# Tiles 4 to 9: half of g turned by TensorE instead of in blocks; queries and keys of batch 3 turned by VectorE

## The chip, the core and the metric

The kernel runs on one core of one Trainium2 chip. The metric is the device time of one execution in microseconds. Five engines work at once, each through its own instruction stream in order: TensorE (PE; its weight loads are PEld), VectorE (DVE), ScalarE (ACT), GpSimd (POOL) and SyncE (SP), which here issues nearly all DMAs.

## The reference

Three parts follow each other: attention of a global and a banded local part, a dense expert, and a soft mixture of 8 experts. All data are float32.

```python
# attention: batch 4, heads 8, 512 local and 32 global positions, head 64
s_g  = scale * q_g @ concat(k_g, k_l).T          # global queries see everything
s_ll = scale * q_l @ k_l.T, kept where |i - j| <= 32
s_lg = scale * q_l @ k_g.T                       # local queries: band and global keys
x = concat(softmax(s_g) @ v, softmax(s_lg, s_ll) @ v)     # (2176, 512)
# dense expert
h = x @ w_in ; g = max(0.01 h, h) ; y = g @ w_out         # 512 -> 2048 -> 512
# soft mixture: 8 experts with 4 slots each
logits = y @ phi                                  # (2176, 32)
d = softmax over tokens ; c = softmax over slots
slots = d.T @ y ; out = c @ expert_mlp(slots)     # w1, relu, w2 for each expert
```

## The kernel before

The 2176 tokens are 17 tiles of 128 (0 to 15 local, four for each batch; 16 holds the global ones). For a tile `b_X` turns the attention output, and `b_H(t, f)` computes a quarter f of h by 12 matmuls of 512 columns (`hp`) and writes g through ScalarE. The logits of a tile need g turned (contraction over its 2048 columns). There are two ways for that:

- `b_L(t, f)`: TensorE transposes a quarter of g in four 128x128 pieces (`gtp`), VectorE or ScalarE brings it to `gT`.
- `blocks(t, f, gs)`, for the tiles in `BLK` (4 to 14): VectorE transposes each quarter in 32x32 blocks (L703, `gb<-g`), and for each two quarters 16 copies of 32x256 move the blocks to their places (L712). `MOVE` gives all 16 of the first half (f 0 and 1) to GpSimd and shares those of the second half (f 2 and 3): 6 GpSimd, 5 VectorE, 5 ScalarE.

Then comes the tile's chain of logits: `b_D1` copies the logits to `lp` (VectorE L744); `b_D2` sums them on TensorE (L750), VectorE takes the maximum (L754), ScalarE the exponential `st` (L759), VectorE copies a part of `st` (L760); `b_D3` transposes `st` on TensorE (L795) and VectorE makes `d` (L782); `b_U` multiplies `d` with g (`up`, L805), and VectorE adds that to `uacc` (L810).

`l_items` lists these steps. `b_items` sets the steps of tile t - 1 between the half quarters of H of tile t. Where t - 1 is in `BLK`, D1 stands behind the second quarter, and three halves of H stand between D2 and D3. Where it isn't, `b_L` stands there first, D1 comes later, and one half of H stands between D2 and D3.

Attention goes by 16 pairs (b, i) of two heads. `load_qk` loads queries and keys (`qn`, `kn`, two buffers each). `a_T` has TensorE transpose each in four pieces (`kTp`, `qTp`), ScalarE brings them to `kT` (four buffers, kept until the global softmax `g_S` has read them) and `qT` (two; with the scale), and VectorE copies the windows `kw` (L403, L404). `a_S` computes scores (`sc`), VectorE adds the mask and takes maxima (L444), ScalarE takes exponentials (L452); `a_E` transposes these (`etp`) and VectorE copies them to `eT` (L473); `a_V` multiplies with values (`vw`), whose global rows GpSimd copies (L200). The steps of attention for batches 2 and 3 are merged with the H of tiles 4 to 10. `gtp`, `kTp`, `qTp`, `etp` and `xtp` share two PSUM banks ("tp"), `sc` and the `gl` of `g_S` two others.

The order on each engine is not that of the code: a scheduler sets it at build, with a time model of its own, so an edit in one place can move rows in others.

Of the kernel before, what the change touches and what calls it, by code (L numbers as in the profile page):

```python
# [8 lines left out]
F32 = mybir.dt.float32  # L9
# [11 lines left out]
def kernel(  # L21
# [15 lines left out]
    nc = tc.nc  # L37
    B, H, S, D = q_l.shape
# [3 lines left out]
    P = 128  # L42
# [5 lines left out]
    NTT = B * NT + 1  # L48
# [10 lines left out]
    def bank(tag, name, bufs):  # L59
        return ps.tile([P, 512], F32, tag=tag, name=name, bufs=bufs)  # L60

    def tp(name):
        return bank("tp", name, 2)
# [93 lines left out]
    def load_qk(b, i, ts=(None, None)):  # L157
        for src, nm, t in ((k_l, "kn", ts[0]), (q_l, "qn", ts[1])):
            if t is None:
                t = sa.tile([P, NT, 2, D], F32, tag=nm, name=nm, bufs=2)  # L160
            for h in range(2):
                nc.sync.dma_start(
                    out=t[:, :, h, :], in_=src[b, 2 * i + h].rearrange("(t p) d -> p t d", p=P)
                )
            nat[nm, b, i] = t
# [215 lines left out]
    def a_T(b, i):  # L381
        qn, kn = nat.pop(("qn", b, i)), nat.pop(("kn", b, i))
        for src, dst, nm, bf in ((kn, kT, "kT", 4), (qn, qT, "qT", 2)):
            pt = tp(nm + "p")
            if b == 0:
                warm(pt)
            for T in range(NT):
                nc.tensor.transpose(
                    pt[:, P * T:P * T + P], src[:, T].rearrange("p h d -> p (h d)"), ident
                )  # L390
            t = sa.tile([P, S], F32, tag=nm, name=nm, bufs=bf)
            nc.scalar.activation(  # L392
                out=t, in_=pt, func=AF.Copy, scale=scale if nm == "qT" else 1.0,
            )
            dst[b, i] = t
        kt = kT[b, i]
        HW = NW // 2
        kwin[b, i] = []
        for hf in range(2):
            kw = sa.tile([P, HW, P], F32, tag="kw", name="kw", bufs=3)  # L400
            src = kt[:, 32 * HW * hf:32 * HW * hf + 96]
            src = bass.AP(src.tensor, src.offset, [src.ap[0], [32, HW], [1, 96]])
            nc.vector.tensor_copy(kw[:, :, 0:96], src)  # L403
            nc.vector.tensor_copy(  # L404
                kw[:, :, 96:128],
                kgT[:, i, 32 * b:32 * b + 32].unsqueeze(1).to_broadcast([P, HW, 32]),
            )
            kwin[b, i].append(kw)
# [7 lines left out]
    def a_S(b, i):  # L416
# [3 lines left out]
        sm = sa.tile([P, NT, 2], F32, tag="sm", name="sm", bufs=2)  # L420
        rs = sa.tile([P, NT, 2], F32, tag="rs", name="rs", bufs=2)
        es = []
        bks = [bank("sc", f"sc{e}", 2) for e in range(2)]
        if b == 0:
            for bk in bks:
# [12 lines left out]
        for e in range(2):  # L438
            bk = bks[e]
            s = sa.tile([P, S + SG], F32, tag="se", name="se", bufs=4)[:, 0:S].rearrange(  # L440
                "p (t k) -> p t k", t=NT
            )
            for T in range(NT):
                nc.vector.tensor_tensor_reduce(  # L444
                    out=s[:, T, :], in0=bk[:, P * T:P * T + P],
                    in1=mask[:, 0 if T == 0 else 2 if T == NT - 1 else 1, :],
                    scale=1.0, scalar=-3.0e38, op0=ALU.add, op1=ALU.max,
                    accum_out=mx[:, e, T:T + 1],
                )
            nc.vector.tensor_scalar_mul(nmx[:, e], mx[:, e], -1.0)  # L450
            for T in range(NT):
                exp_last[0] = nc.scalar.activation(  # L452
                    out=s[:, T, :], in_=s[:, T, :], func=AF.Exp,
                    bias=nmx[:, e, T:T + 1], accum_out=sm[:, T, e:e + 1],
                ).ins
            es.append(s)
        nc.vector.tensor_scalar_add(sm, sm, 1e-9)
# [182 lines left out]
    gt = {}  # L640
    ms = {}
    seq = [(b, T) for b in range(B) for T in range(NT)] + [None]
    BLK = range(4, NTT - 2)
    MOVE = "P" * 16, "PPPPPPDDDDDAAAAA"
    gp = []

# [22 lines left out]
    def b_H(t, f, half=None):  # L669
# [10 lines left out]
        w = wi[f]  # L680
# [8 lines left out]
            return  # L689
        gs = gt[t][:, 512 * f:512 * f + 512]  # L690
        nc.scalar.activation(out=gs, in_=hp, func=AF.Prelu, alpha=0.01)  # L691
        if t in BLK:
            blocks(t, f, gs)

    gbl = {}
# [20 lines left out]
    def b_L(t, f, ev=None):  # L716
        g = gt[t]
        pt = tp("gtp")
        for c in range(4):
            o = 512 * f + P * c  # L720
            nc.tensor.transpose(pt[:, P * c:P * c + P], g[:, o:o + P], ident)  # L721
        gT = part("gT")
        (ev or (nc.vector.tensor_copy if f % 2 and not (t >= 6 and f in (1, 3, 9)) else nc.scalar.copy))(
            gT, pt
        )
        lst[t, f] = gT.rearrange("p (c t) -> p c t", c=4)
# [135 lines left out]

    def l_items(t):
        return ([(0.0, lambda: None), (0.6, lambda: b_M(t, range(2)))] if t in BLK else [
            (0.9, lambda: (b_L(t, 0), b_L(t, 1))),
            (0.9, lambda: (b_L(t, 2), b_L(t, 3))),
        ]) + [
            (1.3, lambda: b_D1(t)),
            (0.3, lambda: b_D2(t)),
            (0.1, lambda: b_D3(t)),  # L870
            (1.0, lambda: b_U(t)),
        ]
# [454 lines left out]
```

## Time and profile before

| what | value |
|---|---|
| median of 3 runs | 519.07 us (516.73 to 519.13) |
| the profiled execution's own time | 516.28 us |
| its span, first to last instruction | 514.2 us |
| TensorE busy | 464.5 us, 90% of the span |
| VectorE, ScalarE, GpSimd busy | 301.2, 248.7, 181.1 us |
| mean granted TensorE clock | 0.962 |

The span is the profiled execution without what lies around it (2.1 us). Busy time of TensorE counts matmuls that are pipelined, so it is not the share of its peak. The granted clock is 1 at 2.4 GHz and 0.5 at 1.2 GHz. Attention of batches 2 and 3 with tiles 4 to 9 lies at about 205 to 345 us, the tiles without attention at 345 to 450 us, and the mixture behind that.

### The profile page before, as it was taken

What the parts mean: (1) busy time and instruction counts of PE and PEld (TensorE: products, weight loads), DVE (VectorE), ACT (ScalarE), POOL (GpSimd) and SP (SyncE); (2) the same over time, 40 slices, a digit from 0 to 9 for tenths busy, and PEclk for the clock granted to TensorE, in tenths of its full rate; (3) what the DMA queues carried; (4) which work ended last, traced back from release to release, by engine and by line L of the source; (5) the groups of instructions that cost most, each with busy time, mean ns of one, the idle gap of its engine ahead of it and who ended that gap; (6) DMA issues with size and microseconds to landing.
All of it is one profiled execution on the core that took longest, in us unless ns stands there. A gap on an engine that the chain in (4) does not pass through costs nothing.

```text
span 514.2 us, 13727 instructions
## 1 busy us (share of the span) xinstructions
PE 464.5 (90%) x5279; PEld 322.2 (63%) x5279; DVE 301.2 (59%) x996; ACT 248.7 (48%) x762; POOL 181.1 (35%) x345
## 2 busy tenths in 40 slices
PE   8976988978999989689898899999999999999994
PEld 5644766556775657456675667677777777633353
DVE  4586769759576663866766975656555541312422
ACT  4787878759654163444525473144433442300222
POOL 2066688443202015206263636516656620000000
PEclk9978899979998999879999999999999999999998
DMA  9998767799755750602480500229620059999987
GB/s 178 235 231 229 212 216 297 209 303 275 189 116 107 169 114 1 131 8 56 127 149 9 108 8 0 84 83 399 256 83 2 0 196 342 385 378 377 302 249 207
DMA packets 122397, 90.25 MB, mean 176 GB/s; under 512 B 75804, under 2 KB 101212, under 8 KB 122332
## 3 DMA queue, kind: packets, MB, share of 16 engines
q1 hardware_dynamic: 119660, 88.33, 60.2%
q10 hardware_dynamic: 2672, 1.05, 0.8%
q8 instruction: 41, 0.67, 0.6%
q14 instruction: 24, 0.20, 0.1%
HBM read 76.68 MB, written 8.65 MB: 166 GB/s over the span
## 4 chain that ended last, share of the span: by engine, by line
PE 60%; DVE 13%; ACT 7%; DMA 5%; issue 3%; POOL 2%; SPq 0%; ACTq 0%; POOLq 0%; DVEq 0%
PE hp L684 29%; PE ehp L1167 3%; PE up L805 3%; PE lg L735 3%; ACT se L452 2%; PE gtp L721 2%; PE sc L432 2%; DMA rraw<-in_moe_w_out_dram 2%; DVE se L444 2%; DMA rraw<-in_moe_w_in_dram 2%; PE po L489 2%; PE sop L1243 1%; POOL wn L259 1%; PE etp L471 1%; PE sop L1221 1%
## 5 line engine op out<-in xcount | busy, mean ns | idle before, releaser
L684 PE MATMUL hp<-wi,xxh 128*128 128x512 f32 x512 | 166.5, 407 | 7.1 <-ACT g L691 3.6
L712 POOL COPY g<-gb 32x256 f32<-32x256 f32 x242 | 97.6, 403 | 95.8 <-DVE gb L703 37.5
L684 PEld LDWEIGHTS hp<-wi,xxh 128*128 128x128 f32 x512 | 92.8, 191 | 41.2 <-issue 12.0
L684 PE MATMUL hp<-wi,xxl 128*128 128x512 f32 x256 | 101.5, 397 | 0.0
L452 ACT ACTIVATE se<-se,nmx 128x128 f32<-128x128 f32 x128 | 49.6, 390 | 24.2 <-DVE nmx L450 21.4
L691 ACT ACTIVATE g<-hp 128x512 f32<-128x512 f32 x60 | 35.7, 594 | 47.6 <-PE hp L684 46.9
L684 PEld LDWEIGHTS hp<-wi,xxl 128*128 128x128 f32 x256 | 48.7, 190 | 12.1 <-issue 0.8
L703 DVE STREAM_TRANSPOSE gb<-g 128x512 f32<-128x512 f32 x44 | 30.9, 706 | 19.4 <-ACT g L691 19.0
L200 POOL COPY vw<-vw 32x1664 f32<-32x1664 f32 x10 | 15.7, 1574 | 70.1 <-DMA vw<-in_v_g_dram 39.2
L259 POOL TENSOR_TENSOR wn<-wn,rraw 128x256 int32<-128x256 int32 x32 | 26.3, 836 | 32.6 <-DMA rraw<-in_moe_w_in_dram 23.4
L432 PE MATMUL sc<-kw,qT 64*32 64x128 f32 x1024 | 29.3, 292 | 1.1 <-issue 0.7
L444 DVE CUSTOM_DVE_ANT_0 se<-sc,mask 128x128 f32<-128x128 f32 x128 | 28.7, 282 | 1.4 <-PE sc L432 1.2
L471 PE MATMUL etp<-identr,se 128*128 128x128 f32 x128 | 23.1, 301 | 5.3 <-ACT kT L392 4.0
L259 POOL TENSOR_TENSOR wo<-wo,rraw 128x256 int32<-128x256 int32 x23 | 18.1, 800 | 25.5 <-DMA rraw<-in_moe_w_out_dram 4.5
L712 ACT COPY g<-gb 32x256 f32<-32x256 f32 x55 | 22.1, 402 | 9.2 <-DVE cs L788 4.1
L489 PE MATMUL po<-vw,eT 128*32 128x64 f32 x1024 | 24.0, 227 | 2.4 <-DMA vw<-vw 1.5
L249 ACT ACTIVATE rraw<-rraw 128x256 int32<-128x256 uint32 x55 | 23.2, 435 | 5.9 <-DMA rraw<-in_moe_w_in_dram 5.1
L432 PEld LDWEIGHTS sc<-kw,qT 64*32 64x32 f32 x1024 | 20.2, 112 | 7.7 <-issue 4.0
L403 DVE COPY kw<-kT 128x672 f32<-128x672 f32 x32 | 19.2, 638 | 9.0 <-ACT kT L392 8.8
L759 ACT ACTIVATE st<-lg,nm 128x128 f32<-128x128 f32 (+1 forms) x16 | 6.0, 373 | 38.2 <-DVE nm L758 34.5
L489 PEld LDWEIGHTS po<-vw,eT 128*32 128x32 f32 x1024 | 18.4, 113 | 9.7 <-issue 7.3
L452 ACT ACTIVATION_READ_ACCUMULATOR se<-se,nmx 128x1 f32 x128 | 24.1, 188 | 0.0
(227 smaller groups left out, 818.1 us busy)
## 6 DMA issues: line engine op xcount, KB each, us to landing
ew<-in_moe_w_dram SPq DMA_DIRECT2D x23, 1024.0 KB, 8.6
rraw<-in_moe_w_in_dram SPq DMA_DIRECT2D x32, 256.0 KB, 3.6
vw<-in_v_l_dram SPq DMA_DIRECT2D x60, 112.0 KB, 3.5
rraw<-in_moe_w_out_dram SPq DMA_DIRECT2D x23, 256.0 KB, 5.3
ew<-in_moe_w_dram SPq DMA_DIRECT2D x9, 512.0 KB, 9.6
ew<-in_moe_w_dram SPq DMA_DIRECT2D x17, 256.0 KB, 5.6
wo_f<-wo SPq DMA_DIRECT2D x16, 256.0 KB, 3.4
vn<-in_v_l_dram SPq DMA_DIRECT2D x4, 1024.0 KB, 6.1
```

The lines of the kernel that those rows point to most:

```text
L249: nc.scalar.activation(out=m, in_=lo, func=AF.Copy, scale=2.0 ** -29)
L259: nc.gpsimd.tensor_tensor(out=di, in0=di, in1=m, op=ALU.add)
L403: nc.vector.tensor_copy(kw[:, :, 0:96], src)
L432: nc.tensor.matmul(bks[e][32 * u:32 * u + 32, P * T:P * T + P], qt[64 * e:64 * e + 64, 32 * U:32 * U + 32], kw[win(U) // (NW // 2)][64 * e ...
L444: nc.vector.tensor_tensor_reduce(out=s[:, T, :], in0=bk[:, P * T:P * T + P], in1=mask[:, 0 if T == 0 else 2 if T == NT - 1 else 1, :], sca ...
L452: exp_last[0] = nc.scalar.activation(out=s[:, T, :], in_=s[:, T, :], func=AF.Exp, bias=nmx[:, e, T:T + 1], accum_out=sm[:, T, e:e + 1],).ins
L471: nc.tensor.transpose(pt[:, P * T:P * T + P], es[e][:, T, :], ident)
L489: nc.tensor.matmul(pov[32 * u:32 * u + 32, T, e, :], ets[e][:, 32 * U:32 * U + 32], vw[:, win(U), e, :], start=True, stop=True,)
L684: nc.tensor.matmul(hp, a[:, k, :], w[c][:, k, :], start=(k == 0 and n == 0), stop=(k == KD - 1 and n == 2),)
L691: nc.scalar.activation(out=gs, in_=hp, func=AF.Prelu, alpha=0.01)
L703: nc.vector.transpose(out=gb[:, f % 2], in_=gs)
L712: copy(dst[32 * c:32 * c + 32, :, a], src[32 * a:32 * a + 32, :, c])
```

## The change

The set `BLK` now holds tiles 10 to 14. A new set `HALF` holds 4 to 9: there quarters 0 and 1 are still turned in blocks (all moves on GpSimd), and quarters 2 and 3 by `b_L`. These tiles now take the other order of steps in `b_items`.

For batch 3 the loads of queries and keys go in runs of 32 floats (128 bytes): eight 32-partition DMAs for a pair where four of 128 partitions with runs of 256 bytes stood. The tile then holds 32x32 blocks in such places that one VectorE transpose of 128x512 gives `kT` or `qT`; the four TensorE transposes and ScalarE's copy are gone. The scale that this copy gave to the queries moves into the exponential.

```diff
--- before.py
+++ after.py
@@ -158,7 +158,19 @@
         for src, nm, t in ((k_l, "kn", ts[0]), (q_l, "qn", ts[1])):
             if t is None:
                 t = sa.tile([P, NT, 2, D], F32, tag=nm, name=nm, bufs=2)
+            if b >= 3:
+                t = t.rearrange("p t h d -> p (t h d)").rearrange("p (w d) -> p w d", d=32)
             for h in range(2):
+                if b >= 3:
+                    for c in range(2):
+                        g = 64 * h + 32 * c
+                        nc.sync.dma_start(
+                            out=t[g:g + 32],
+                            in_=src[b, 2 * i + h, :, 32 * c:32 * c + 32].rearrange(
+                                "(w k) d -> k w d", k=32
+                            ),
+                        )
+                    continue
                 nc.sync.dma_start(
                     out=t[:, :, h, :], in_=src[b, 2 * i + h].rearrange("(t p) d -> p t d", p=P)
                 )
@@ -381,6 +393,11 @@
     def a_T(b, i):
         qn, kn = nat.pop(("qn", b, i)), nat.pop(("kn", b, i))
         for src, dst, nm, bf in ((kn, kT, "kT", 4), (qn, qT, "qT", 2)):
+            if b >= 3:
+                t = sa.tile([P, S], F32, tag=nm, name=nm, bufs=bf)
+                nc.vector.transpose(out=t, in_=src.rearrange("p w d -> p (w d)"))
+                dst[b, i] = t
+                continue
             pt = tp(nm + "p")
             if b == 0:
                 warm(pt)
@@ -420,6 +437,7 @@
         sm = sa.tile([P, NT, 2], F32, tag="sm", name="sm", bufs=2)
         rs = sa.tile([P, NT, 2], F32, tag="rs", name="rs", bufs=2)
         es = []
+        sc_q = scale if b >= 3 else 1.0
         bks = [bank("sc", f"sc{e}", 2) for e in range(2)]
         if b == 0:
             for bk in bks:
@@ -447,11 +465,11 @@
                     scale=1.0, scalar=-3.0e38, op0=ALU.add, op1=ALU.max,
                     accum_out=mx[:, e, T:T + 1],
                 )
-            nc.vector.tensor_scalar_mul(nmx[:, e], mx[:, e], -1.0)
+            nc.vector.tensor_scalar_mul(nmx[:, e], mx[:, e], -sc_q)
             for T in range(NT):
                 exp_last[0] = nc.scalar.activation(
                     out=s[:, T, :], in_=s[:, T, :], func=AF.Exp,
-                    bias=nmx[:, e, T:T + 1], accum_out=sm[:, T, e:e + 1],
+                    bias=nmx[:, e, T:T + 1], scale=sc_q, accum_out=sm[:, T, e:e + 1],
                 ).ins
             es.append(s)
         nc.vector.tensor_scalar_add(sm, sm, 1e-9)
@@ -640,7 +658,8 @@
     gt = {}
     ms = {}
     seq = [(b, T) for b in range(B) for T in range(NT)] + [None]
-    BLK = range(4, NTT - 2)
+    BLK = range(10, NTT - 2)
+    HALF = range(4, 10)
     MOVE = "P" * 16, "PPPPPPDDDDDAAAAA"
     gp = []
 
@@ -689,7 +708,7 @@
             return
         gs = gt[t][:, 512 * f:512 * f + 512]
         nc.scalar.activation(out=gs, in_=hp, func=AF.Prelu, alpha=0.01)
-        if t in BLK:
+        if t in BLK or t in HALF and f < 2:
             blocks(t, f, gs)
 
     gbl = {}
@@ -862,7 +881,7 @@
 
     def l_items(t):
         return ([(0.0, lambda: None), (0.6, lambda: b_M(t, range(2)))] if t in BLK else [
-            (0.9, lambda: (b_L(t, 0), b_L(t, 1))),
+            (0.0, lambda: None) if t in HALF else (0.9, lambda: (b_L(t, 0), b_L(t, 1))),
             (0.9, lambda: (b_L(t, 2), b_L(t, 3))),
         ]) + [
             (1.3, lambda: b_D1(t)),
```

What moves in the order of instructions is shown at three places. Numbers behind a tile's name are buffers.

The first is TensorE at tile 3's chain of logits, while the scores of batch 2's last pair are computed. Before:

```order
L471 MATMUL etp<-identr,se 128x128 x8
L750 MATMUL lg<-lp,s_77 128x128
L388 MATMUL kTp<-identr,kn 128x128 x4
L388 MATMUL qTp<-identr,qn 128x128 x4
L471 MATMUL etp<-identr,se 128x128 x4
...
L795 MATMUL lg<-identr,st 128x128
...
L471 MATMUL etp<-identr,se 128x128 x2
L805 MATMUL up<-gx,d 32x512 x4
L684 MATMUL hp<-wi,xxh 128x512 x2
L684 MATMUL hp<-wi,xxl 128x512
```

`sc` are those scores, `etp` behind `qTp` the exponentials of the pair before. The change:

```order
L489 MATMUL etp<-identr,se 128x128 x8
L769 MATMUL lg<-lp,s_77 128x128
L405 MATMUL kTp<-identr,kn 128x128 x4
L405 MATMUL qTp<-identr,qn 128x128 x4
L740 MATMUL gtp<-identr,g 128x128 x4
L814 MATMUL lg<-identr,st 128x128
...
L450 MATMUL sc_3421<-kw,qT 32x128
L824 MATMUL up<-gx,d 32x512 x4
L703 MATMUL hp<-wi,xxh 128x512 x2
L703 MATMUL hp<-wi,xxl 128x512
L703 MATMUL hp<-wi,xxh 128x512 x2
L703 MATMUL hp<-wi,xxl 128x512
```

The second `etp` has gone behind, tile 4's `gtp` stands in its place, and the transpose of `st` and `up` come before most of the scores.

The second place is VectorE at tile 4's chain, from `lp` on, where batch 2's global softmax (`gmx`, `gnmx`) is computed too. Before:

```order
L744 COPY lp<-lg 128x128
L703 STREAM_TRANSPOSE gb<-g 128x512
L473 COPY eT<-etp 128x512
L661 SCALAR_TENSOR_TENSOR xxl<-xtp,xxh 128x512
L526 TENSOR_REDUCE gmx<-gl 128x1 x2
L754 TENSOR_REDUCE nm<-lg 128x1
L758 TENSOR_TENSOR nm<-nm 128x1
L527 TENSOR_REDUCE gmx<-gg 128x1
L763 TENSOR_TENSOR al<-nm 128x1
L527 TENSOR_REDUCE gmx<-gg 128x1
L528 TENSOR_REDUCE gnmx<-gmx 128x1
L760 COPY st<-lg 32x128
```

The change:

```order
L763 COPY lp<-lg 128x128
L420 COPY kw<-kT 128x7x96
L491 COPY eT<-etp 128x512
L398 STREAM_TRANSPOSE kT<-kn 128x512
L545 TENSOR_REDUCE gmx<-gg 128x1
L773 TENSOR_REDUCE nm<-lg 128x1
L545 TENSOR_REDUCE gmx<-gg 128x1
L398 STREAM_TRANSPOSE kT<-kn 128x512
L546 TENSOR_REDUCE gnmx<-gmx 128x1
L777 TENSOR_TENSOR nm<-nm 128x1
L546 TENSOR_REDUCE gnmx<-gmx 128x1
L515 TENSOR_TENSOR xn<-po,rs 128x4x128
```

Two key transposes of batch 3 and window copies now stand between `lp` and the second `nm`; the block transpose is gone.

The third place is TensorE at the same chain, from the matmul on `lp` (D2) to the transpose of `st` (D3). Before, two rows of H repeat where lines are left out:

```order
L750 MATMUL lg<-lp,s_77 128x128
L684 MATMUL hp<-wi,xxh 128x512 x2
L684 MATMUL hp<-wi,xxl 128x512
L521 MATMUL gg<-kgT,qgT 32x32 x8
L684 MATMUL hp<-wi,xxh 128x512 x2
L684 MATMUL hp<-wi,xxl 128x512
...
L489 MATMUL po<-vw,eT 32x64 x8
L388 MATMUL kTp<-identr,kn 128x128 x4
L388 MATMUL qTp<-identr,qn 128x128 x4
L489 MATMUL po<-vw,eT 32x64 x23
L795 MATMUL lg<-identr,st 128x128
L471 MATMUL etp<-identr,se 128x128 x8
```

The change:

```order
L769 MATMUL lg<-lp,s_77 128x128
L539 MATMUL gg<-kgT,qgT 32x32 x4
L507 MATMUL po<-vw,eT 32x64 x28
L450 MATMUL sc_3863<-kw,qT 32x128 x16
L489 MATMUL etp<-identr,se 128x128 x4
L450 MATMUL sc_3864<-kw,qT 32x128 x9
L489 MATMUL etp<-identr,se 128x128 x4
L814 MATMUL lg<-identr,st 128x128
L450 MATMUL sc_3864<-kw,qT 32x128 x7
L507 MATMUL po<-vw,eT 32x64 x4
L740 MATMUL gtp<-identr,g 128x128 x4
L450 MATMUL sc_4145<-kw,qT 32x128 x7
```

No `hp` is left between D2 and D3; the second half of the values, scores and `etp` stand there, and tile 5's `gtp` follows.

## Rows read from the trace of the kernel before

**Rows 1.** The page: busy microseconds, share of span and instructions of each engine.
```profile
PE 464.5 (90%) x5279; PEld 322.2 (63%) x5279; DVE 301.2 (59%) x996; ACT 248.7 (48%) x762; POOL 181.1 (35%) x345
```
**Rows 2.** Windows (us, engines' busy time with instructions, granted clock, DMA share, GB/s).
```profile
215.00:226.00 11.00, 6.95 (x85) 3.44 (x83) 8.52 (x40) 6.06 (x26) 3.53 (x7) 0.54 0.22 49
...
205.00:345.00 140.00, 126.70 (x1780) 89.99 (x1780) 95.83 (x326) 64.31 (x216) 56.87 (x123) 0.96 0.30 64
345.00:417.00 72.00, 72.00 (x480) 53.66 (x479) 41.22 (x110) 28.60 (x75) 44.12 (x110) 1.00 0.39 147
```
**Rows 3.** TensorE's waits, 210 to 350 us: total, times, longest.
```profile
PE etp L471 <- ACT kT L392: 4.0, 1, 4.0
...
PE up L805 <- DVE d L782: 1.6, 1, 1.6
PE lg L750 <- DMA vw<-in_v_l_dram: 1.5, 1, 1.5
```
**Rows 4.** TensorE in order of time: start, duration, work, and idle before it.
```profile
213.30 0.49 PE L750 MATMUL lg<-lp,s 128*128 128x128 f32 x2 [1.52 <-DMA vw<-in_v_l_dram]
...
219.86 1.11 PE L471 MATMUL etp<-identr,se 128*128 128x128 f32 x4 [4.05 <-ACT kT L392]
...
224.37 1.92 PE L805 MATMUL up<-gx,d 128*32 128x512 f32 x8
...
243.06 0.66 PE L388 MATMUL kTp<-identr,kn 128*128 128x128 f32 x4
243.55 0.60 PE L388 MATMUL qTp<-identr,qn 128*128 128x128 f32 x4
...
248.80 1.06 PE L805 MATMUL up<-g,d 128*32 128x512 f32 x8 [1.62 <-DVE d L782]
```
**Rows 5.** Costs by operation and shape, 205 to 345 us: busy, mean ns, idle before.
```profile
L703 DVE STREAM_TRANSPOSE gb<-g 128x512 f32<-128x512 f32 x23 | 16.0, 705 | 5.8 <-ACT g L691 5.4 <-ACT al L764 0.3
...
L712 DVE COPY g<-gb 32x256 f32<-32x256 f32 x30 | 13.0, 433 | 0.5
L712 ACT COPY g<-gb 32x256 f32<-32x256 f32 x30 | 12.1, 402 | 5.6 <-DVE nmx L450 3.9 <-DVE cs L788 1.4
...
L392 ACT ACTIVATE kT<-kTp 128x512 f32<-128x512 f32 x6 | 3.6, 593 | 4.1 <-PE kTp L388 4.1
...
L759 ACT ACTIVATE st<-lg,nm 128x128 f32<-128x128 f32 x6 | 2.2, 365 | 14.8 <-DVE nm L758 11.1 <-DVE gmx L527 3.7
...
L760 DVE COPY st<-lg 32x128 f32<-32x128 f32 x6 | 1.7, 284 | 1.7 <-ACT st L759 1.7
```
**Rows 6.** VectorE in order of time.
```profile
212.37 0.71 DVE L703 STREAM_TRANSPOSE gb<-g 128x512 f32<-128x512 f32 x1
...
215.02 1.18 DVE L450 TENSOR_SCALAR nmx<-mx 128x4 f32<-128x4 f32 x1
...
242.82 1.33 DVE L703 STREAM_TRANSPOSE gb<-g 128x512 f32<-128x512 f32 x2
...
244.50 1.21 DVE L403 COPY kw<-kT 128x672 f32<-128x672 f32 x2
...
248.76 1.27 DVE L473 COPY eT<-etp 128x512 f32<-128x512 f32 x2
```
**Rows 7.** ScalarE in order of time.
```profile
216.44 1.23 ACT L712 COPY g<-gb 32x256 f32<-32x256 f32 x3
...
219.23 0.57 ACT L392 ACTIVATE kT<-kTp 128x512 f32<-128x512 f32 x1
...
239.92 0.68 ACT L532 ACTIVATE gs<-gl,gnmx 128x512 f32<-128x512 f32 x1
```
**Rows 8.** The issue queue of SyncE, and how long key loads take to land.
```profile
207.72 4.09 SPq L191 DMA_DIRECT2D vw<-in_v_l_dram  x6
...
215.25 0.94 SPq L162 DMA_DIRECT2D kn<-in_k_l_dram  x2
...
DMA to landing us min/median/max: 2.3/2.7/3.5
```
**Rows 9.** GpSimd in order of time.
```profile
214.60 1.57 POOL L200 COPY vw<-vw 32x1664 f32<-32x1664 f32 x1 [9.17 <-DMA vw<-in_v_l_dram]
```

## The prediction

> **What bounds the kernel now.** The page's busy times come first: TensorE has 90% of the span, VectorE 59% [rows 1]. That is an average, so the windows come next. From 345 to 417 us TensorE is busy for all of 72.0 us at full clock; from 205 to 345 us, where the change sits, for 126.7 of 140 [rows 2]. So this stage holds 13.3 us in which TensorE stands, and each microsecond of TensorE's work that is added or taken away, or of standing that comes or goes, passes to the end: nothing behind it has slack. The list of TensorE's waits says what ends the standing: one wait of 4.0 us for ScalarE's copy of keys, one of 1.6 us for `d`, one of 1.5 us, then smaller ones [rows 3]. (The 1.5 us are put down to a DMA, but the matmul waits for VectorE's `lp`.) TensorE in order of time puts the largest close together: 1.52 us ahead of 213.30, some smaller ones, 4.05 us ahead of 219.86; the third is tile 4's `up` at 248.80 [rows 4]. The first group costs more than its idle time: from 215 to 226 us the granted clock is 0.54 [rows 2], and `up` there takes 1.92 us against 1.06 for the same columns at 248.80 [rows 4]. At 1.2 GHz lie some 6.3 us of work, from 219.86 to about 226.2; half of that, 3.2 us, is lost.
>
> So the group at 212 to 226 us costs about 6.3 us of idle (1.5 + 0.8 + 4.0) and 3.2 us of clock, tile 4's `up` 1.6 us, and the rest 13.3 - 6.3 - 1.6 = 5.4 us.
>
> **TensorE's own work.** `b_L` adds two groups of four transposes in each of six tiles, 12 groups; the four pairs of batch 3 lose two each, 8 groups. A group costs 0.49 us, from `kTp` at 243.06 to `qTp` at 243.55; up to 0.58 elsewhere [rows 4]. Four more groups: **+2.2 us** (1.9 to 2.4), all on the path.
>
> **The other engines' work.** VectorE loses in each of six tiles two block transposes of 0.705 us and five moves of 0.433, ScalarE five moves of 0.402 [rows 5], GpSimd six moves of about as much. VectorE gains eight transposes of queries and keys, costed as the same instruction on the same shape, 0.705 us, and two copies from PSUM (tiles 4 and 5) near 0.64 [rows 6]: -21.5 + 5.6 + 1.3 = -14.6 us. ScalarE gains ten such copies and loses eight, 0.593 each [rows 5]: -12.1 + 1.2 = -10.9 us. None of this counts by itself; it counts where TensorE's wait ends with that engine. The scale in the exponential is an operand of the same instruction: nothing (ScalarE's slack would hide a nanosecond on it anyway).
>
> **The stall at 212 to 226 us.** TensorE waits until ScalarE's `kT` copy at 219.23 frees a bank [rows 4, 7]. Ahead of that copy ScalarE does five of tile 4's moves and eight exponentials; three moves take 1.23 us, and four exponentials fill the 1.56 us from 217.67 to 219.23 [rows 7]. VectorE does two block transposes around `lp` and five moves [rows 5, 6]. All these moves go, and the new order has the `kT` copy between the two sets of exponentials. The first set can then start near 212.8, when the maxima are done (the 212.37 of the first block transpose [rows 6] and a small instruction): copy at 214.4, done at 214.9, against 219.8. What is late next is tile 3's `st`: ScalarE does four more exponentials (to 216.6), `st` 0.37, VectorE 0.28 [rows 5]: 217.3, while TensorE is through with `gtp` at 215.5. I count waits of 0.9, 0.2, 0.5 and 1.7 us, 3.3 in all, and `up` at about 218.1 where 224.37 stands. These waits are spread, and TensorE stays busy over half of the time, as it did around the 1.62 us wait, where the clock stayed full; so I take no fall. 9.5 - 3.3: **-6.2 us**. Bounds: -3 if the clock falls once or half of the wait stays, -8 if nearly all goes.
>
> **Tile 4's chain.** Before, three halves of H and two groups of transposes lie between D2 and D3, and TensorE stands for 1.62 us. After, no H is left there. VectorE's queue, counted from the end of `gl`: `gmx`, `xxl`, two keys turned, `gmx`, `eT`, three window copies, `eT`, two more keys turned, 12 passes of full size at 0.6 to 0.7 us [rows 5, 6], 7.7 us, with the small ones some 9.2 us, until ScalarE may begin the global softmax; its first exponential takes 0.68 us [rows 7] and only then frees a bank for the scores. TensorE has work for 6.1 us meanwhile (three quarter tiles' worth of transposes, logits and values, one quarter of H), and the queue has started half a microsecond earlier: about 3.3 us of waiting. Behind D3, VectorE does two `eT`, four mask passes, window copies and `d`, some 3.2 us, before `up`; TensorE has 1.2 us of work: 2.0 more. 5.3 against 1.6: **+3.7 us**. Bounds: +0.5 if the queue is shorter when it gets there, +7 if keys come late (below). TensorE would stand for over 2 us here in one piece, as at 213 to 216 us, behind which the clock fell; one stretch at 1.2 GHz, most of it in the shadow of waiting: **+1.0 us** (0 to 3.2).
>
> **The other waits, 5.4 us before.** Those for `eT` and key copies at the transposes of batch 3 (some 1.7 us) go with them. For tile 6 I find 1.8 us, since scores, `eT` and maxima of two sets stand ahead of `nm`; tiles 7 to 9 about 0.5, 0.4 and 0.9 (at tile 9 only transposes of attention's output cover D2 to D3); 0.8 for the rest: 4.4. **-1.0 us** (-3 to +2).
>
> **Loads.** Each pair has eight issues of 512 runs where four stood. An issue of keys takes 0.47 us and one of values 0.68 [rows 8], so the queue gains 2 to 3 us a pair; values issued behind land later by that, hidden by GpSimd, which has waited 9.17 us for them already [rows 9], as long as it isn't late for `a_V`. I cost that at nothing; without cover, 2 us a pair.
>
> Sum: 2.2 - 6.2 + 3.7 + 1.0 - 1.0 = **-0.3 us**. The profiled execution's own time is 516.28 us, so 516.0; it lies 0.5% under the median of 519.07, on whose scale this is 518.8 us. Over or under 0.5% (2.6 us) a measurement of this kernel can tell from no change.
>
> **The rivals.**
>
> *The second stall doesn't form: faster.* For it speaks that VectorE has 14.6 us less to do, and that my queue adds passes as if none could slip ahead of its place. Then +3.7 + 1.0 become about +0.3, the sum is -4.3 us: 514.7 us. Against it: the rows of the new order have no H between D2 and D3. It decides whether VectorE reaches the last key within 6 us of `gl`.
>
> *Keys come late: slower.* VectorE's third and fourth key transposes of batch 3 use buffers that its first two free. Eight issues follow at 0.47 to 0.68 us each [rows 8], 3.8 to 5.4 us, and the last lands 2.3 to 3.5 us behind [rows 8]: 6.1 to 8.9 us after the first transpose, which VectorE's own queue reaches after about 7. From 7 us on, VectorE stands with the softmax and `nm` behind it. Runs of 128 bytes were not traced here; the nearest are 256. With landing 1 to 2 us longer, 3 us more, and another stretch of slow clock, 1.7: +4.4 us, 523.2 us. The Trainium skill, "DMA: Bandwidth & Descriptors", section "Specifications", gives 512 bytes as the least transfer for full line rate and so speaks against shorter runs; both kernels are under that, and rows 8 show what 256 bytes cost, not 128.
>
> *The first stall stays: slower.* GpSimd's copy of values, 1.57 us from 214.60 [rows 9], ends at 216.17; VectorE's tiny `nmx` began at 215.02 and took 1.18 us, to 216.20 [rows 6]. So VectorE stood still until GpSimd was through. With values 2 us later this copy falls at 217, on the instructions ahead of `st`: 1.6 us more there, and with them the clock falls once. The gain shrinks to 3.0: +2.9 us, 521.7 us. The Trainium skill, "SBUF — State Buffer", section on the single rule of contention, says the port pair that the two engines share is locked for a whole instruction and the other fully blocks; the trace agrees (1.18 us). By that rule alone the time would be this rival's.
>
> *The change does little:* if the waits did not hang on the moves, only +2.2 us would be left: within 0.5%, 521.3 us.
>
> **How the numbers follow.** No measurable change, the sum and the last rival: 0.42. Faster: 0.34, the first rival, or a first stall that goes wholly. Slower: 0.24, half each for late keys and a stall that stays. The predicted time is the sum's, 518.8 us; its own range, 516.2 to 521.4. Taking in the rivals' centres with their bounds, 513 to 523.5 us leaves out one in ten on each side.
>
> **What would show it.** Right: at tile 3's `up` the clock near 1 and `up` 6 us earlier; a wait of over 2 us between tile 4's D2 and D3, ended by ScalarE's `gs`; 48 `gtp` transposes more, at 0.12 to 0.15 us each. Wrong: no wait there; or VectorE waiting for `kn`; or `etp` still waiting 4 us for `kT`. Most likely to be wrong are the two stalls' sizes: each is worked out along queues that shift by a microsecond with any instruction ahead.

## The result, and the profile after

The changed kernel took 522.16 us (median of 12 runs, 519.87 to 525.87), the kernel before 519.08 in the same comparison: ratio 1.0087, interval 1.0063 to 1.0112, so 4.5 us slower (3.3 to 5.8). A second comparison, on another chip, gave 1.0090 (1.0059 to 1.0121). Ratios leave out executions that took over 1.5% longer than the fastest of their kernel; the changed kernel had none. No measurable change was forecast.

The page of the changed kernel, busy microseconds, share of the span and instructions, beside [rows 1]:

```profile
PE 474.1 (91%) x5295; PEld 326.3 (63%) x5295; DVE 284.3 (55%) x964; ACT 236.8 (46%) x734; POOL 166.1 (32%) x309
```

TensorE is busy 9.6 us longer, the three others 11.9 to 16.9 us shorter. Two of the windows of [rows 2], and the two of tile 4's chain (us, busy time of PE, PEld, DVE, ACT and POOL with instructions, granted clock, DMA share, GB/s):

```profile
215.00:226.00 11.00, 8.57 (x143) 5.60 (x147) 8.57 (x27) 6.04 (x25) 1.57 (x1) 1.00 0.77 125
205.00:345.00 140.00, 133.79 (x1714) 94.59 (x1716) 75.71 (x284) 50.27 (x181) 44.34 (x94) 0.96 0.31 62
237.00:250.00 13.00, 10.27 (x175) 7.22 (x174) 11.15 (x43) 4.12 (x18) 4.38 (x11) 0.84 0.51 123
250.00:265.00 15.00, 15.00 (x124) 10.20 (x124) 6.79 (x21) 4.15 (x17) 0.66 (x2) 0.79 0.21 42
```

From 215 to 226 us the clock is 1.00 where it was 0.54: the first stall went as forecast. But now there is a fall from 237 to 265 us (0.84 and 0.79), where before had none:

```profile
237.00:250.00 13.00, 11.38 (x206) 7.82 (x191) 10.63 (x31) 6.99 (x22) 9.15 (x20) 1.00 0.29 67
250.00:265.00 15.00, 14.45 (x229) 10.77 (x228) 9.87 (x39) 6.07 (x21) 5.37 (x13) 1.00 0.47 114
```

From 205 to 345 us TensorE stands for 6.2 us where it stood for 13.3, and still the stage ends later. Its waits, 210 to 350 us (total, times, longest; beside [rows 3]):

```profile
PE sc L450 <- ACT gs L550: 1.7, 1, 1.7
PE lg L814 <- DVE st L779: 1.5, 1, 1.5
PE lg L769 <- DMA vw<-in_v_l_dram: 0.9, 1, 0.9
```

The 4.0 us for `kT` are gone. TensorE in order of time (start, duration, work, idle before it), beside [rows 4] (the trace lists scores, `up` and some other float32 matmuls as two each: `up` counts 8 here for 4 in the order of instructions):

```profile
219.82 0.33 PE L814 MATMUL lg<-identr,st 128*128 128x128 f32 x1 [1.55 <-DVE st L779]
...
220.86 1.06 PE L824 MATMUL up<-gx,d 128*32 128x512 f32 x8
...
240.31 0.49 PE L769 MATMUL lg<-lp,s 128*128 128x128 f32 x2 [0.40 <-DVE lp L763]
241.42 0.26 PE L539 MATMUL gg<-kgT,qgT 64*32 64x32 f32 x8 [0.62 <-DVE eT L491]
...
244.32 1.08 PE L450 MATMUL sc<-kw,qT 64*32 64x128 f32 x32 [1.71 <-ACT gs L550]
...
248.21 0.42 PE L814 MATMUL lg<-identr,st 128*128 128x128 f32 x1
...
252.00 1.07 PE L824 MATMUL up<-g,d 128*32 128x512 f32 x3
```

Tile 3's `up` takes 1.06 us at full clock. Tile 4's chain runs from D2 (240.31) over D3 (248.21) to `up` (252.00). In it TensorE waits 0.40, 0.62 and 1.71 us and then runs without a pause; its clock fell at 246 us and was back at 256.2. All these 10.2 us are work at 1.2 GHz: 5.1 us lost. The wait of 1.71 us is for ScalarE's `gs`; what ScalarE waited for stands in VectorE's queue and in ScalarE's:

```profile
241.29 0.69 DVE L398 STREAM_TRANSPOSE kT<-kn 128x512 f32<-128x512 f32 x1
...
242.65 0.71 DVE L398 STREAM_TRANSPOSE kT<-kn 128x512 f32<-128x512 f32 x1 [0.29 <-DMA kn<-in_k_l_dram]
243.28 0.11 DVE L546 TENSOR_REDUCE gnmx<-gmx 128x1 f32<-128x2 f32 x1
```
```profile
243.49 0.69 ACT L550 ACTIVATE gs<-gl,gnmx 128x512 f32<-128x512 f32 x1 [3.38 <-DVE nm L777]
```

The third and fourth key transposes, 0.69 and 0.71 us, and 0.29 us for the key load between them, stand ahead of `gnmx`, and `gnmx` ahead of `gs`. (ScalarE's row names `nm`, which ends at about the same time; the bias of `gs` is `gnmx`.)

What the edits cost by themselves (205 to 345 us, by operation and shape; beside [rows 5]), and the key loads in the list of DMAs (count, KB each, median us from issue to landing):

```profile
L740 PE MATMUL gtp<-identr,g 128*128 128x128 f32 x40 | 6.8, 296 | 0.8 <-ACT gs L556 0.4 <-ACT kT L409 0.3
...
L398 DVE STREAM_TRANSPOSE kT<-kn 128x512 f32<-128x512 f32 x4 | 2.7, 694 | 0.3 <-DMA kn<-in_k_l_dram 0.3
```
```profile
kn<-in_k_l_dram SPq DMA_DIRECT2D x20, 128.0 KB, 3.5
...
kn<-in_k_l_dram SPq DMA_DIRECT2D x16, 64.0 KB, 2.5
```

VectorE's key transposes take 0.69 us, as costed. The whole trace has 112 `gtp` transposes of `g` where before has 64: 48 more, as forecast. The 16 issues of keys in 128 byte runs, half as large, land after 2.5 us in the median; those in 256 byte runs take 3.5 in this list and 2.7 in [rows 8].

**Where the time went.** The stage is cut at the updates (`up`) of tiles 2, 3, 4 and 10, whose starts TensorE in order of time gives; ahead of tile 2's and behind tile 10's both kernels do the same (from tile 10's update to the end of the execution's own time it is 145.0 us in both first profiles). Tile 2's update itself stands anywhere from 187 to 195 us in the 14 profiles, and from 189 to 193 in the three of the changed kernel. The clock is that of the 30 us from 45 to 75 us behind tile 2's update, in which tile 4's chain lies (windows).

| kernel | 2 to 3 | 3 to 4 | 4 to 10 | clock | ratio to before |
|---|---|---|---|---|---|
| before | 34.06 | 24.43 | 122.52 | 1.00 | 1 |
| before, second profile | 35.62 | 23.60 | 123.06 | 1.00 | |
| after | 27.90 | 31.14 | 124.82 | 0.83 | 1.0087 |
| after, second profile | 27.86 | 30.57 | 123.52 | 0.89 | |
| after, third profile | 28.64 | 33.77 | 124.38 | 0.77 | 1.0090 |
| e1_half_only | 30.06 | 25.79 | 126.55 | 1.00 | 1.0064 |
| e2_turn_only | 34.05 | 26.60 | 125.93 | 0.89 | 1.0076 |
| e3_cover | 29.14 | 24.73 | 123.36 | 1.00 | 0.9938 |
| e3_again | 28.46 | 24.86 | 123.39 | 1.00 | 0.9915 |
| e4_two_pairs | 30.10 | 28.27 | 124.27 | 1.00 | 1.0003 |
| e5_keep | 30.01 | 28.12 | 124.11 | 1.00 | 1.0003 |
| e6_cover_hold | 28.36 | 24.22 | 128.54 | 1.00 | 1.0026 |
| e7_turn_hold | 34.04 | 23.75 | 129.46 | 0.94 | 1.0160 |
| e10_half_cover | 29.64 | 24.22 | 124.93 | 1.00 | 0.9969 |

(In four of these executions the first 15 us behind tile 2's update run at 0.89, which puts 1.7 us on the first column: the second profile of before, e1, e4 and e5.) So the change gains 5 to 6 us ahead of tile 3's update, gives 6 to 9 back up to tile 4's, and 1 to 2 more behind it (all against the first row).

### The profile page after: what moved, and what is told of

Its sections match the earlier page's. It is cut to its first block, busy times and chain, and to the rows that moved or that the text cites. A ratio compares the mean times of both kernels' runs of the same rounds, so it can differ in the third digit from the quotient of the medians.

```text
span 520.1 us, 13664 instructions
## 1 busy us (share of the span) xinstructions
PE 474.1 (91%) x5295; PEld 326.3 (63%) x5295; DVE 284.3 (55%) x964; ACT 236.8 (46%) x734; POOL 166.1 (32%) x309
## 4 chain that ended last, share of the span: by engine, by line
PE 67%; DVE 7%; ACT 5%; DMA 5%; issue 2%; POOL 2%; SPq 1%; DVEq 0%; ACTq 0%; POOLq 0%
PE hp L703 30%; PE sc L450 4%; PE gtp L740 3%; PE ehp L1186 3%; PE up L824 3%; PE lg L754 3%; PE po L507 3%; DMA rraw<-in_moe_w_in_dram 2%; PE etp L489 2%; DMA rraw<-in_moe_w_out_dram 2%; PE sop L1262 2%; PE op L1286 1%; POOL wn L271 1%; PE sop L1240 1%; DMA kn<-in_k_l_dram 1%
## 5 line engine op out<-in xcount | busy, mean ns | idle before, releaser
L731 POOL COPY g<-gb 32x256 f32<-32x256 f32 x206 | 82.5, 400 | 79.6 <-DVE gb L722 66.9
L722 DVE STREAM_TRANSPOSE gb<-g 128x512 f32<-128x512 f32 x32 | 22.3, 704 | 25.7 <-ACT g L710 19.2
L450 PE MATMUL sc<-kw,qT 64*32 64x128 f32 x1024 | 34.5, 297 | 1.7 <-ACT gs L550 1.7
L450 PEld LDWEIGHTS sc<-kw,qT 64*32 64x32 f32 x1024 | 23.0, 114 | 10.1 <-issue 5.1
L507 PEld LDWEIGHTS po<-vw,eT 128*32 128x32 f32 x1024 | 18.0, 113 | 13.6 <-issue 6.8
L491 DVE COPY eT<-etp 128x512 f32<-128x512 f32 x28 | 18.9, 686 | 13.8 <-PE etp L489 13.4
L489 PEld LDWEIGHTS etp<-identr,se 128*128 128x128 f32 x128 | 15.7, 152 | 7.9 <-issue 3.7
```

The costliest lines, as they stand in the source:

```text
L450: nc.tensor.matmul(bks[e][32 * u:32 * u + 32, P * T:P * T + P], qt[64 * e:64 * e + 64, 32 * U:32 * U + 32], kw[win(U) // (NW // 2)][64 * e ...
L489: nc.tensor.transpose(pt[:, P * T:P * T + P], es[e][:, T, :], ident)
L507: nc.tensor.matmul(pov[32 * u:32 * u + 32, T, e, :], ets[e][:, 32 * U:32 * U + 32], vw[:, win(U), e, :], start=True, stop=True,)
L722: nc.vector.transpose(out=gb[:, f % 2], in_=gs)
L731: copy(dst[32 * c:32 * c + 32, :, a], src[32 * a:32 * a + 32, :, c])
```

## Experiments

**Each part alone.** e1_half_only: queries and keys of batch 3 stay as before. e2_turn_only: tiles 4 to 9 stay in blocks.

```diff
 e1_half_only, against the changed kernel
-            if b >= 3:
+            if b >= 9:
...
-        sc_q = scale if b >= 3 else 1.0
+        sc_q = scale if b >= 9 else 1.0
 e2_turn_only, against the changed kernel
-    BLK = range(10, NTT - 2)
-    HALF = range(4, 10)
+    BLK = range(4, NTT - 2)
+    HALF = ()
```

> Tiles 4 to 9 as in the changed kernel (second half of g turned by TensorE), queries and keys of batch 3 as before, so TensorE turns 8 groups more than in the changed kernel, about 4.5 us by the two traces. Theory A (the order: tiles 4 to 7 have no H between D2 and D3 and the matmuls stand in more and smaller pieces; that gives the clock fall and the longer work): the same order of tiles, so no faster than the changed kernel, 522 to 527 us, and a fall of the clock somewhere in tiles 4 to 6. Theory B (VectorE's key transposes in 128 byte runs stand ahead of the global softmax and make the wait and the fall): wait and fall are gone, 517 to 520 us.

> Batch 3 turned by VectorE from 128 byte runs, tiles 4 to 9 wholly in blocks as before. Theory A: H stays between D2 and D3, TensorE saves 8 groups (4.5 us), the first stall at 212 to 226 us stays: 514 to 517 us, faster than before. Theory B: VectorE, with all block transposes and moves and the key transposes as well, makes TensorE wait for the global softmax: 520 to 525 us.

e1: ratio 1.0064 (1.0029 to 1.0099), 522.4 us on the first comparison's scale. The time is at the edge of theory A's, the place isn't: no fall in tiles 4 to 6 (clock 1.00), and what is longer lies behind tile 4's update, 126.55 against 122.5 us. The execution profiled took 514.85 us where the median is 519.30, so it shows the loss only in part; what the clock cost over all twelve is worked out below. By count TensorE has twelve groups more here and none less, some 6 us; that this is the loss was not tested. e2: 1.0076 (1.0038 to 1.0113), 523.0 us: theory A fails, B's time stands, though TensorE does not wait for the global softmax as B has it. Its rows (us, TensorE's busy time, clock; then TensorE's waits) say what it waits for. They are of an execution of 523.26 us; the median of all twelve is 521.60:

```profile
191.57:378.15 186.58, 172.94 (x2011) 0.95 0.36 98
206.57:236.57 30.00, 24.03 (x381) 0.83 0.57 100
236.57:266.57 30.00, 27.97 (x384) 0.89 0.26 61
```
```profile
PE etp L489 <- DVE eT L491: 4.2, 3, 2.1
PE etp L489 <- ACT kT L409: 3.7, 1, 3.7
```

The first stall stays (3.7 us for `kT`, clock 0.83), VectorE keeps its blocks, gets the transposes as well, and is waited for at `eT`. TensorE loses eight groups and stands instead. Neither part is a gain alone.

**H between D2 and D3.** e3_cover gives tiles 4 to 9 the order of items that block tiles have.

```diff
-            if t - 1 in BLK:
+            if t - 1 in BLK or t - 1 in HALF:
```

> The changed kernel, but the items of tiles 4 to 9 in the order that block tiles have: three halves of H behind D2, ahead of D3. Theory A: the waits of tile 4's chain (2.7 us), the fall of the clock behind them (5.1 us) and some of the price of D2 and D3 between small matmuls go: 5 to 8 us under the changed kernel, 514 to 517 us, under before. Rival C (TensorE's added transposes and the broken up scores are the whole loss, whatever stands between D2 and D3): within 1.5 us of the changed kernel, 521 to 524 us.

> e3_cover again, on one chip with the changed kernel. Theory A: 1.0 to 1.8% under the changed kernel, ratio to before 0.990 to 0.997; in its stage neither a wait of over 1.2 us nor a fall of the clock in tile 4's chain. Rival C (the order of H between D2 and D3 doesn't matter): within 0.4% of the changed kernel.

Ratio 0.9938 (0.9903 to 0.9973), and 0.9915 (0.9881 to 0.9949) beside the changed kernel, of which it is 0.983 (512.52 to 521.34 us): theory A, at the upper end of its size. Tile 3's to tile 4's update takes 24.7 to 24.9 us, and what is left of the wait for `gs` is 0.34 us (TensorE in time in e3_cover; then windows of the stage and of the 30 us in e3_again). One sign of theory A is missed: at tile 3, which keeps its order, a wait of 1.55 us for `st` stays in e3_again.

```profile
244.92 1.06 PE L450 MATMUL sc<-kw,qT 64*32 64x128 f32 x26 [0.34 <-ACT gs L550]
```
```profile
188.44:365.15 176.71, 172.75 (x2058) 0.99 0.39 104
233.44:263.44 30.00, 29.50 (x456) 1.00 0.36 79
```

This version beats both kernels, by 0.6 to 0.9% of before.

**The fall, and what makes the wait.** e5_keep puts dummy matmuls where TensorE stood; e4_two_pairs takes the last two pairs' key transposes off VectorE.

```diff
 e5_keep, in g_S
+            if b == 2 and e == 1:
+                for _ in range(10):
+                    nc.tensor.matmul(
+                        bg[:, P:512], identr, identr.unsqueeze(1).to_broadcast([P, 3, P]),
+                        start=True, stop=True, skip_group_check=True,
+                    )
 e4_two_pairs, in load_qk, a_T and a_S
-            if b >= 3:
+            if b >= 3 and i < 2:
```

> The changed kernel with ten dummy matmuls of 384 columns (about 1.6 us, their results not read) behind the second global logits of batch 2, in the stretch of tile 4's chain where TensorE stood. Theory A (the clock falls behind the standing, and costs 5.1 us): the clock stays full through 240 to 260 us, 517 to 519 us. Rival D (the dummies only add or shift work, the fall has another cause): the clock falls as before or later, 521.5 to 524 us.

> The changed kernel with only the first two pairs of batch 3 turned by VectorE; the other two are loaded and turned as before, so two key transposes of VectorE (1.3 us) and the load of keys they wait for no longer stand ahead of the global softmax of tile 4's chain, and TensorE turns 4 groups more (2.2 us). Theory B2 (these keys make the wait for the global softmax, 1.5 to 1.7 us, and the fall behind it): wait under 0.5 us, full clock from 237 to 265 us, 1 to 3 us under the changed kernel. Theory A2 (without H between D2 and D3 something else stands there): a wait of 1 us or more remains in the chain, time within 1.5 us of the changed kernel or over it.

Both 1.0003 (0.9967 to 1.0038, and 0.9964 to 1.0042), some 4.4 us under the changed kernel: theory A, 0.2 us over its range, and theory B2, with a larger gain than it had. Windows of the 30 us, and in each the place of the former wait in TensorE's time, e5 first:

```profile
234.06:264.06 30.00, 29.01 (x380) 1.00 0.36 78
```
```profile
240.83 2.01 PE L546 MATMUL gg<-identr 128*128 128x384 f32 x10
```
```profile
237.52:267.52 30.00, 28.85 (x403) 1.00 0.32 78
```
```profile
245.43 1.06 PE L450 MATMUL sc<-kw,qT 64*32 64x128 f32 x26
```

The clock stays full in both. In e5 the dummies do no useful work (2.0 us from 240.83 on; the scheduler shifts the order around them a little), and the kernel is faster for it. In e4 the scores follow without a wait, though TensorE has four groups more to do. Tile 3's to tile 4's update is 28.1 and 28.3 us against 30.6 to 33.8. So the two key transposes, with the load between them, make the wait, the fall comes with the wait, and without the fall most of the loss is gone. e4 keeps a wait of 1.7 us for `gs` elsewhere, at batch 3's own global softmax, without a fall behind it; so one wait of this size does not always bring a fall.

The timed executions bear this out beyond single profiles. Each has its span and its mean granted clock on record. The span times what the clock lacks to 1 is an estimate of the time that the clock cost, on the high side where TensorE stood. Against the kernel before on the same chip its mean is 2.9 us more in the changed kernel (23.1 and 20.2, second comparison), 2.4 us less in e4 (17.8 and 20.2) and 3.5 us less in e5 (15.6 and 19.1). What is left of the time is 2.0, 2.9 and 3.5 us more than in before. So the clock is what e4 and e5 win back, and they pay part of it in work. In e1_half_only the clock costs 1.6 us less than in before and the rest is 5.0 us more: its loss is not one of the clock.

**Broken runs of scores.** In the stage TensorE's small matmuls grew too. Scores (`sc`) in before, after, e2_turn_only and e7_turn_hold, 185 to 380 us (by shape: busy, mean ns of one, idle before):

```profile
L432 PE MATMUL sc<-kw,qT 64*32 64x128 f32 x448 | 11.0, 295 | 0.7 <-issue 0.7
```
```profile
L450 PE MATMUL sc<-kw,qT 64*32 64x128 f32 x448 | 14.9, 290 | 1.7 <-ACT gs L550 1.7
```
```profile
L450 PE MATMUL sc<-kw,qT 64*32 64x128 f32 x448 | 16.9, 310 | 0.2 <-DVE kw L420 0.2
```
```profile
L452 PE MATMUL sc<-kw,qT 64*32 64x128 f32 x442 | 10.4, 295 | 0.0
```

The same 448 matmuls (442 recorded in the last), of nearly the same mean, take 11.0, 14.9, 16.9 and 10.4 us, some of it in stretches at half clock (with these counted half it is 9.7 us in before and 13.1 in after). From the last piece ahead of tile 3's update on, TensorE does them in 7 pieces in before and in 16 in after and e2. A whole set in before, and pieces of one in after:

```profile
246.02 1.16 PE L432 MATMUL sc<-kw,qT 64*32 64x128 f32 x64
```
```profile
273.90 0.85 PE L450 MATMUL sc<-kw,qT 64*32 64x128 f32 x30
274.68 0.33 PE L814 MATMUL lg<-identr,st 128*128 128x128 f32 x1
274.94 0.44 PE L450 MATMUL sc<-kw,qT 64*32 64x128 f32 x14
275.31 0.33 PE L606 MATMUL gxt<-identr,xg 128*128 128x128 f32 x1
275.48 0.60 PE L740 MATMUL gtp<-identr,g 128*128 128x128 f32 x4
276.01 0.41 PE L450 MATMUL sc<-kw,qT 64*32 64x128 f32 x6
276.35 1.07 PE L824 MATMUL up<-g,d 128*32 128x512 f32 x8
```

From start to the next start 30 matmuls take 0.78 us, 14 take 0.37 and 6 take 0.34; 64 in one run take 1.16. e6_cover_hold and e7_turn_hold hold each set behind the last H half issued ahead of it, which leaves 9 and 7 pieces:

```diff
-        for T, u, e in seq_ if b > 1 else sorted(seq_, key=lambda x: x[2]):
+        hold = tc.issue_after(ms["hp"]) if b >= 3 else ExitStack()
+        with hold:
+            for T, u, e in seq_ if b > 1 else sorted(seq_, key=lambda x: x[2]):
...
-                nc.tensor.matmul(
+                ms["hp"] = nc.tensor.matmul(
                     hp, a[:, k, :], w[c][:, k, :],
                     start=(k == 0 and n == 0), stop=(k == KD - 1 and n == 2),
-                )
+                ).ins
```

> e3_cover with the scores of batch 3 held behind the last H half that the program has issued, which leaves 9 pieces of scores on TensorE from tile 4 on where e3_cover has 14 (the kernel before 7, the changed one 16). Theory E (a broken run of scores costs TensorE time, about 0.3 us a piece by the traces so far): scores take about 8.5 us where they took 10.0, and the time is 1 to 2 us under e3_cover, ratio to before 0.990 to 0.992. Rival F (pieces cost nothing, the scores were longer for other reasons): scores stay near 10 us, ratio 0.993 to 0.995.

> e2_turn_only with the same hold: 7 pieces of scores where e2_turn_only has 16. Theory E: scores fall from 11.7 us to about 8.3, and the time by 2 to 4 us, ratio to before 1.000 to 1.004, if the waits of that kernel stay. Rival F: scores stay above 11 us, ratio 1.006 to 1.009.

The scores went down as theory E has it (e7: 10.4 us; e6: 9.9 where e3_cover has 12.8, in the same view), and both kernels got slower than what they were made from, 1.0026 (0.9992 to 1.0061) and 1.0160 (1.0109 to 1.0212): outside both theories' times. The stage of e7:

```profile
188.80:376.05 187.25, 170.38 (x2011) 0.94 0.36 97
```
```profile
PE etp L491 <- ACT se L472: 2.5, 1, 2.5
PE gpo L595 <- DVE geg L583: 2.4, 1, 2.4
```

Against e2 TensorE is busy 2.6 us less and stands 3.2 us longer (16.9 and 13.6). The two rows are waits of e7 that e2's list does not have: the first is for the exponentials (`se`) of a held set. So the hold does two things, it joins the pieces and it makes the scores late for what follows them, and e6 and e7 cannot tell a price of the pieces from that. What they show is that fewer pieces got this way are no gain.

**The turn, with H in place.** e10_half_cover is e3_cover with the `b >= 9` of e1_half_only.

> e3_cover with queries and keys of batch 3 as in the kernel before, so TensorE turns 8 groups more (4.5 us), scores in 10 pieces. Theory A (H between D2 and D3 is what counts, and the turn by VectorE is a gain of TensorE's own work once that cover is there): slower than e3_cover by 2.5 to 4.5 us, ratio to before 0.999 to 1.003. Rival G (VectorE's turn is itself a loss, as e2_turn_only alone would suggest): as fast as e3_cover or faster, ratio 0.986 to 0.994.

Ratio 0.9969 (0.9927 to 1.0011), between the two theories: with H in place the turn by VectorE is worth 0.3 to 0.5% if anything (the intervals of e10 and e3_cover overlap), less than the 4.5 us of TensorE's work that it takes away.

**How far executions differ.**

> The changed kernel once more, one look: how much of the stage from tile 2's to tile 10's update (183.9 us in the profile of after, 181.0 before) is the kernel's and how much one execution's. Theory A: the clock falls behind the wait in tile 4's chain again (some 10 us at 1.2 GHz from about 246 us), stage 183 to 185 us. Rival H (the fall was this one execution's): full clock there, stage 178 to 180 us.

> The changed kernel again, beside the next kernel on the same chip. If the loss is the kernel's: ratio to before 1.005 to 1.011, as at first (1.0087). If a good part of it was the chip's or the day's: 1.000 to 1.004, which is what its second profile (stage 181.95 us against 181.01 before) would suggest.

> The kernel before once more, one look, for how far two executions of one kernel differ: stage from tile 2's to tile 10's update 180 to 182 us (181.0 in the first), the two falls of the stage at the same places (the stall at 212 to 226 us alone), while the time to tile 2's update may differ by some us (190.3 before, 193.0 and 189.0 in the two of the changed kernel).

The windows of the stage and of the 30 us in the first, second and third profile of the changed kernel:

```profile
192.96:376.82 183.86, 176.61 (x2058) 0.97 0.37 100
237.96:267.96 30.00, 27.27 (x333) 0.83 0.34 76
```
```profile
189.04:370.99 181.95, 174.95 (x2058) 0.98 0.38 101
234.04:264.04 30.00, 27.53 (x340) 0.89 0.34 76
```
```profile
188.94:375.73 186.79, 180.06 (x2059) 0.95 0.37 98
233.94:263.94 30.00, 27.34 (x312) 0.77 0.34 75
```

The standing is the same within 0.6 us (7.25, 7.00 and 6.73 of the stage), the fall comes each time, and its length differs: 10.2, 6.8 and 13.7 us at 1.2 GHz, of which half, 5.1, 3.4 and 6.8 us, is lost. In the first two it begins 1.7 and 2.0 us behind the end of the wait for `gs`, in the third 0.3 us after that wait has begun. The third profile has 0.89 in the 30 us ahead as well. The second's stage of 181.95 us lies between the ranges of theory A and rival H, and this single execution took 515.95 us, within the range of before on that chip (513.15 to 521.44). The ratio of 1.0090 is what the loss being the kernel's had put. The second profile of before, an execution of 515.30 us, has a stage of 182.28 us, 0.3 over what was put, and besides the stall a further fall, 3.4 us long, right behind tile 2's update.

## Why the prediction was wrong

The likeliest case, no measurable change at 518.8 us, did not come. The time lies in the outer range (513 to 523.5 us) and over the sum's own (516.2 to 521.4), and the sign is that of the two slower rivals. By place, the three profiles against the first of before, the forecast holds at tile 3 (-6.2, -6.2 and -5.4 us; put at -6.2) and about holds behind tile 4's update (+2.3, +1.0 and +1.9; put at +1.2 for TensorE's own work and the other waits). At tile 4's chain it does not: +6.7, +6.1 and +9.3, put at +4.7. (By the prediction's own terms its first three rivals come to 514.4, 523.5 and 522.0 us, each 0.3 us from the time that it gives; nothing hangs on that.)

- **The stall at 212 to 226 us, -6.2: right.** Tile 2's to tile 3's update is 6.2 us shorter in the first pair of profiles, the waits there are 0.93, 0.18, 0.32 and 1.55 us, and the clock is full. The rival that this stall stays is out, and so is the one that the waits do not hang on the moves, though its 521.3 us lie near: in e2, which keeps the moves, the wait of 3.7 us stays.
- **Tile 4's chain, waits +3.7, clock +1.0: this step failed, in its clock term.** The waits came out shorter than put, 2.7 us in place of 5.3 (the one for `gs` 1.71 where over 2 was put): the 2.0 put behind D3 did not come, since TensorE was busy from 244.32 us on, at half clock from 246. The clock term rested on "one stretch at 1.2 GHz, most of it in the shadow of waiting". TensorE did not wait in the shadow: it had work for all of the 10.2 us, and lost 5.1 (3.4 and 6.8 in two more executions), over the bound of 3.2 each time. The pattern that the term was taken from was misread, too: at 213 to 216 us TensorE did not stand in one piece. Ahead of the fall at 215.9 us it stood for 1.52 and 0.77 us with work between and behind them, and the wait of 4.05 us began only as the clock fell. Here it stood for 0.40, 0.62 and 1.71 us. Where the fall is kept away by dummy matmuls (e5) or with two key transposes fewer and four groups more (e4), over 4 of the 4.5 us are gone.
- **Late keys, as a rival at 523.2: right in place, wrong in mechanism.** VectorE waited only 0.29 us for a key load. The transposes themselves, 1.4 us ahead of `gnmx`, delayed the global softmax: without them the wait is gone (e4). On loads of 128 byte runs that rival's price, and the rule of the Trainium skill, "DMA: Bandwidth & Descriptors", section "Specifications", which it was set beside, did not come to bear: the issues, each half as large, land no later than those of 256 byte runs in [rows 8].
- **TensorE's own work +2.2, "all on the path": mis-sized as well.** Twelve groups more and eight fewer are there, at 0.53 us from start to start (275.48 to 276.01) where 0.49 was put. But scores took 3.9 us more (14.9 against 11.0; 3.4 more at full clock), and TensorE's busy time in the stage, tile 2's to tile 10's update, rose from 167.7 to 176.6 us while its standing fell from 13.3 to 7.25. At full clock that is 6.9 us of work more, 4.7 over this term, while the other waits (next point) came out 3.9 under theirs; that the two nearly cancel in the sum is luck. They may belong together. If half of what TensorE works at 1.2 GHz is taken off, the stage is 177 to 179 us in before, after, e2, e4, e5, e6 and e7, whatever TensorE's share of it; it moves with the order of the items (e3: 174 to 175; e10: 176) and in e1 (181). This speaks for work and waits being no two terms to be added, as the step took them: small matmuls in pieces can fill time in which TensorE would stand. It is argued, not shown, since e6 and e7 also made the scores late.
- **Other waits -1.0:** -4.9 in the profile. From 205 to 345 us TensorE stands for 6.2 us, 3.0 of them at tile 3 and 2.7 in tile 4's chain, which leaves 0.5 of 5.4. The longer work of the point above outweighs that: from tile 4's update on the stage is 1 to 2 us longer.
- **Loads and the scale in the exponential, 0:** nothing in the trace speaks against it.

**What stays open.** The three profiles of the changed kernel give 2.6 us more than the two of before in the stage on average (184.2 against 181.6), the timed runs 4.5. What the fall costs differs by 3.4 us between executions, and five profiles are few. Over the second comparison's executions the estimate above puts 2.9 us on the clock and 2.0 on the rest. Why the fall lasts 7 us once and 14 us another time was not tried.

## What to carry to other kernels

Ask of a wait not only how long it is but what TensorE does behind it: 2.7 us of standing, in three waits within 5 us, cost 3 to 7 us more here, because a dense run of work followed at half clock, and 2 us of dummy matmuls in place of the longest were a gain. When work is moved to an engine with slack, look at what small instruction stands behind it in that engine's queue (`gnmx`, 0.1 us), and who waits for that. When tiles change their method, carry over the order of items too: three halves of H between D2 and D3 turned this change from 0.9% slower into 0.6 to 0.9% faster.

## What the runs showed of the hardware

Small matmuls that overlap on TensorE (448 of 295 ns each take 11.0 us in before) cost more when their run is broken up: 64 scores in one run took 1.16 us, 30 took 0.78, 14 took 0.37 and 6 took 0.34. The global logits of one batch took 1.09 us where the 16 that the trace lists for both heads stood in one run (in before, at 236.48 us), and 1.06 us for the 8 of each head alone (in after, at 314.60 and 321.24 us). Switching to them costs as well: in e4 the next matmul of H starts 0.23 us behind one of H (241.09 to 241.32 us), the global logits 0.32 us behind one (241.77 to 242.09). In before, at full clock from 190 to 380 us, 15 steps from H to matmuls on a part of the array (`lg`, `gl`, `gg`, `po`, `sc`, `up`, `gpo`) took 0.32 to 0.33 us, and 20 from H to other matmuls on the whole array 0.23 to 0.24. The Trainium skill, "TensorEngine Tiling (Array Packing)", section "Tiling Modes", says that a change of tiling mode drains TensorE; these 0.09 us agree with that.
